# Three edits to an attention and two-MoE kernel: attention ranks, planned cost of the activation sums, address of the stationary operands

## The chip, the cores and the metric

The kernel runs on one core of a Trainium2 chip. The metric is the device time of one execution in microseconds (us). TensorE (PE) does matmuls, and its weight loads (PEld) overlap with them; VectorE is DVE, ScalarE is ACT, GpSimd is POOL, and SyncE (SP) issues all DMAs.

## The reference, cut to what matters

```python
def reference(**kwargs):
    attn_out = _attn_ref(q, k, v)          # 2 x 8 heads, 576 positions, head size 64
    x = attn_out.transpose(0, 2, 1, 3).reshape(1152, 512)
    x = _moe_ref(x, w_gate, w1, w2)         # 8 experts
    return _moe2_ref(x, domain_probs, w1, w2)   # 4 experts

def _attn_ref(q, k, v):
    # softmax attention over positions averaged in fours, repeated four times,
    # plus softmax attention in a window of 7 positions (|i - j| < 4)
    return out_up + out_local

def _moe_ref(x, w_gate, w1, w2):
    P = np.exp(logits - logits.max())       # then 8 rounds of row and column normalisation
    for e in range(8):
        out += P[:, e:e + 1] * (np.maximum(x @ w1[e], 0.0) @ w2[e])   # 512 -> 1024 -> 512
    return out
# _moe2_ref: the same with 4 experts and p = domain_probs / row sum
```

## The kernel before, in words

**Numbers.** Activations and weights are held as a high and a low part in a rounded 32-bit format, and each product is three matmuls (high x high, high x low, low x high).

**Stages.** Attention works on eight pairs of heads and writes `xh` and `xl`, the transposed activations. Twelve experts follow, each in two halves (`grp`). A half has a first product (288 columns of moving activations per matmul, stationary weights `w1s` or `w1s_b`; lines 288, 449, 486) and a second one (512 columns of moving `w2s`, stationary hidden activations `ht`; line 653). The first product uses a recursive scheme with seven products in place of eight, so it needs sums of blocks of activations: one level made by `x_sums` (`sh`, `sl`) and a second by `deep_sums` (`sx` and freed places of the other tiles). A sum is two or more elementwise adds on POOL or DVE (lines 1102, 1108, 1158) and a `keep`: an ACT copy to the high part (line 1172; line 1118 in `x_sums`) and a DVE subtraction for the low part.

**Order.** No queue is written by hand. `Plan.add` records a task with an engine, an estimated cost, what it reads and writes, and a due time: the PE time planned so far, plus `slack`. While an attention pair is recorded, `slack` also takes the next of the 44 values of `plan.ranks` (line 1031). `Plan.run` then simulates the engines with those costs. At each step it takes, per engine, the task that can begin earliest, and among equals the one due first. The order so found is the order in each engine's queue, and on the chip each engine runs its queue strictly in that order. There are two plans: the first (attention, half of expert 0's first half) and the second (the rest), which starts with the engines' simulated times of the first.

**The 44 ranks**, by place: 0 and 1 the two POOL adds that average q and k (lines 872, 874); 2 to 8 the windowed scores; 9 to 21 the averaged scores (19 the POOL multiply of line 923); 22 to 24 the normalisation (24 the POOL multiply of line 857); 25 and 26 the two POOL adds that average v (lines 881, 884); 27 to 33 transposes; 34 to 43 values and the split into `xh` and `xl`. The buffers between 0 and 1, and between 25 and 26, are rings of one.

**Costs of sums.** A POOL add of 288 columns is planned at `pool_cost(288)` = 160 + 2.25 x 288 = 808 ns, a DVE one with both inputs in SBUF at `SHARED` = 870 ns.

**Addresses.** `shifted` (line 252) makes a tile 64 floats longer and starts 36 floats in, that is 144 bytes. `own` holds `ht`, four slots of `w1s` and four of `w2s` one behind the other, all with sizes that are multiples of 256 bytes; `w1s_b` is made by `shifted` too. Unshifted, these tiles begin on a multiple of 256 bytes. So all stationary operands of the experts and the moving `w2s` are at 144 of 256; the moving `xh`, `xl`, `sh`, `sl` and `sx` are at 0 or 128 of 256.

Of the kernel before, what the change touches and what calls it, by code (L numbers as in the profile page):

```python
# [9 lines left out]
F32R = mybir.dt.float32r  # L10
# [189 lines left out]
def tile_attention_moe_moe(  # L200
# [13 lines left out]
    nc = tc.nc  # L214
    NPAIR = qk.shape[0]
    S = qk.shape[2] // 2
    NT, DM = out.shape
    HP = DM // 128
    D = 64
    E1, E2 = w1a.shape[0], w1b.shape[0]  # L220
# [7 lines left out]
    U = S // 2  # L228
# [3 lines left out]
    big = ctx.enter_context(tc.tile_pool(name="big", bufs=1))  # L232
# [18 lines left out]

    def shifted(pool, name, n):

        return pool.tile([128, 64 + n], F32R, name=name)[:, 36:36 + n]

    def w1_slots(t):
        return [x.rearrange("p (a k b) -> p a k b", a=2, k=2) for x in slots(t)]

    def w2_slots(t):
        return [x.rearrange("p (a d) -> p a d", a=2) for x in slots(t)]  # L260

    def slots(t):
        return [t[:, j:j + 1024] for j in range(0, t.shape[1], 1024)]

    own = shifted(big, "own", 8 * NT + 8192)
    ht = own[:, 0:8 * NT].rearrange("p (j a n) -> p j a n", j=4, a=2)
    w1s = w1_slots(own[:, 8 * NT:8 * NT + 4096])
    w2s = w2_slots(own[:, 8 * NT + 4096:])
    acc = [big.tile([128, DM], F32, name=f"acc_{n}") for n in range(3)]
    raw = [big.tile([128, DM], F32, name=f"raw_{j}") for j in range(4)]  # L270

# [6 lines left out]
    plan = Plan()  # L278
# [14 lines left out]
    def copy_cost(n):  # L293
        return 190.0 + 0.85 * n

    def pool_cost(n):
        return 160.0 + 2.25 * n
# [91 lines left out]
    T_OF = {(0, 0): (0, 1, 2), (0, 1): (2, 3, 4), (1, 0): (4, 5, 6), (1, 1): (6, 7, 8)}  # L389
    A_OF = {1: ("x", 1, 0), 2: ("x", 1, 2), 4: ("x", 0, 2), 5: ("s", 0), 6: ("s", 1), 7: ("s", 2), 3: ("s", 3)}  # L390
    DEEP = (3, 7, 5, 4, 6, 2, 1)
    SUMS = (2,2,2,1)
    ON_POOL = (0, 2)

    def ready(g, grp, more=0):
        return sum(SUMS[:max(2 * (g % E1) + grp - (g < E1) + more, 0)])


    def x_tiles(b, u, h=None):
# [26 lines left out]
    def part_of(p, k, u):  # L426

        kind, i, *rest = A_OF[p]
        if kind == "x":
            c = i * S + u * U  # L430
            return [a[:, rest[0] + k, c:c + U] for a in (xh, xl)]
        return [a[:, i, k, u * U:u * U + U] for a in (sh, sl)]

    def part_keys(p, u):
        kind, i, *rest = A_OF[p]
        if kind == "x":
            return x_tiles(i, u, rest[0] // 2)
        return [("s", i, j, hl) for j in (2 * u, 2 * u + 1) for hl in range(2)]
# [585 lines left out]
    def warm(n):  # L1024
# [4 lines left out]


    plan.ranks = (
# [4 lines left out]
    )  # L1036
    for i in range(NPAIR):
        plan.step = 0
# [28 lines left out]
    late = ctx.enter_context(tc.tile_pool(name="late", bufs=1))  # L1067
    late.tile([128, 112], F32, name="gap2")
    w1s += w1_slots(shifted(late, "w1s_b", 1024 * 2))
    raw += [late.tile([128, DM], F32, name=f"raw_{j}") for j in range(4, 6)]  # L1070

# [6 lines left out]
    plan = Plan()  # L1078
# [3 lines left out]


    r_sum = Ring([late.tile([128, U], F32, name=f"sum_{j}") for j in range(3)])
    SHARED = 870.0
    LAG = 18000.0

    def x_sums(j, on_pool=False):

        wd = S // 4  # L1090
        c = wd * j
        part = [[r_tmp.new() for _ in range(2)] for _ in range(2)]

        def v(t):
            return t.slot.rearrange("p (k t) -> p k t", k=2)

        for b in (1, 0):
            o = b * S + c
            tiles = range(o // 128, (o + wd - 1) // 128 + 1)
            for h in range(2):  # L1100
                t = part[b][h]
                plan.add("POOL", pool_cost(2 * wd), lambda t=t, o=o, h=h: nc.gpsimd.tensor_tensor(
                    out=v(t), in0=xh[:, 2 * h:2 * h + 2, o:o + wd].bitcast(F32),
                    in1=xl[:, 2 * h:2 * h + 2, o:o + wd].bitcast(F32), op=ALU.add), [("x", n, h) for n in tiles], (t,))

        def two(dst, x, y, op):
            e = nc.gpsimd if on_pool else nc.vector
            plan.add("POOL" if on_pool else "DVE", pool_cost(2 * wd) if on_pool else SHARED, lambda: e.tensor_tensor(
                out=v(dst), in0=v(x), in1=v(y), op=op), (x, y), (dst,))

        (a21, a22), (a11, a12) = part
        two(a22, a21, a22, ALU.add)
        two(a21, a11, a21, ALU.subtract)
        two(a11, a22, a11, ALU.subtract)
        two(a12, a12, a11, ALU.subtract)
        for i, t in enumerate((a22, a11, a21, a12)):
            hi, lo = sh[:, i, :, c:c + wd], sl[:, i, :, c:c + wd]
            plan.add("ACT", copy_cost(2 * wd), lambda t=t, hi=hi: nc.scalar.activation(
                out=hi, in_=v(t), func=ACTF.Copy), (t,), (("s", i, j, 0),), after=own_keys("s", i))
            plan.add("DVE", SHARED, lambda t=t, hi=hi, lo=lo: nc.vector.tensor_tensor(  # L1120
                out=lo, in0=v(t), in1=hi.bitcast(F32), op=ALU.subtract),
                (t, ("s", i, j, 0)), (("s", i, j, 1),), after=own_keys("s", i))
# [3 lines left out]
    def own_keys(kind, i=None):  # L1126
        return [("l2", p, i_, hl) for (p, i_), (k, j) in homes.items() if k == kind and (i is None or i == j)
                for hl in range(2)]
# [3 lines left out]
    for p in DEEP:  # L1132
        kind, i, *_ = A_OF[p]
        own = (part_of(p, 0, 1), kind, i if kind == "s" else (i, 1, _[0] // 2))
# [7 lines left out]
    def home_keys(p, i):  # L1142

        kind, j = homes[p, i]
        if kind == "s":
            return [("s", j, t, hl) for t in (2, 3) for hl in range(2)]
        if kind == "x":
            return x_tiles(*j)
        return []

    def deep_sums(p, on_pool):

        pool = (nc.gpsimd, "POOL", pool_cost(U))
        t = [r_sum.new() for _ in range(3)]

        def sub(eng, dst, x, y, reads, writes, op=ALU.subtract, slack=LAG, after=()):
            e, name, cost = eng
            plan.add(name, cost, lambda: e.tensor_tensor(  # L1158
                out=dst(), in0=x(), in1=y(), op=op), reads, writes, slack=slack, after=after)

        def whole_part(d, u, k):
            hi, lo = part_of(p, k, u)
            sub(pool, lambda: d.slot, lambda: hi.bitcast(F32), lambda: lo.bitcast(F32), part_keys(p, u), (d,), ALU.add)

        def two(dst, x, y, op):
            sub(pool if on_pool else dve, lambda: dst.slot, lambda: x.slot, lambda: y.slot, (x, y), (dst,), op)

        dve = (nc.vector, "DVE", SHARED)

        def keep(i, d):  # L1170
            hi, lo = sums[p][i]
            plan.add("ACT", copy_cost(U), lambda: nc.scalar.activation(
                out=hi, in_=d.slot, func=ACTF.Copy), (d,), (("l2", p, i, 0),), after=home_keys(p, i), slack=LAG)
            sub(dve, lambda: lo, lambda: d.slot, lambda: hi.bitcast(F32), (d, ("l2", p, i, 0)), (("l2", p, i, 1),),
                after=home_keys(p, i))

        whole_part(t[0], 1, 0)
        whole_part(t[1], 1, 1)
        whole_part(t[2], 0, 0)
        two(t[1], t[0], t[1], ALU.add)  # L1180
        two(t[0], t[2], t[0], ALU.subtract)
        two(t[2], t[1], t[2], ALU.subtract)
        keep(0, t[1])
        keep(2, t[0])
        keep(1, t[2])
        whole_part(t[1], 0, 1)
        two(t[1], t[1], t[2], ALU.subtract)
        keep(3, t[1])
# [171 lines left out]
    for q in range(2):  # L1360
        for h in range(2):
            for u in range(2):
                plain_unit(first_w1[2 * h:2 * h + 2], q, 2 * q + h, 1, u)
        for j in range(2):
            x_sums(2 * q + j, 2 * q + j in X_POOL0)
# [9 lines left out]
    def tiles(g, grp, w):  # L1375
# [54 lines left out]
        for i, n in enumerate(ORDER):  # L1430
            if i in SUM_AT and ready(g, grp) + SUM_AT.index(i) < ready(g, grp, 1):
                work.append(lambda k=ready(g, grp) + SUM_AT.index(i): deep_sums(DEEP[k], k in ON_POOL))
            if special and i:
                work.append(lambda i=i: whole_tile(i))
            elif i < (4 if 1 in DEEP[:ready(g, grp, 1)] else 5):
                work += steps(i)
            else:
                rest += steps(i)
# [115 lines left out]
```

## Time and profile before

| | us |
|---|---|
| median of 3 runs | 1172.27 (1172.06 to 1172.35) |
| the profiled execution | 1173.12 |
| its span, first to last instruction | 1171.3 |
| PE busy in the span | 1157.0 |
| POOL busy | 950.7 |
| DVE busy | 838.9 |
| ACT busy | 656.1 |

The profiled execution took 1.8 us outside its span, and was 0.85 us longer than the median of the runs. Matmuls are pipelined and their recorded ends are modelled, so a PE that is 99% busy may still wait: what one matmul costs is read from the chain of waits, where a piece with its count runs from the first start to the next piece. The mean TensorE clock granted was 0.999 of 2.4 GHz.

### The profile page before, as it was taken

The page shows a single profiled execution, that of the slowest core. Times are in us where ns is not written, and L with a number is a line of the kernel's source. Part 1 is how long each engine was busy: PE and PEld are TensorE (multiplying, and loading weights), DVE is VectorE, ACT ScalarE, POOL GpSimd, SP SyncE. Part 2 cuts the span into 40 slices and gives each one's busy share as a digit, 9 for nine tenths or more (in the row PEclk, how much of TensorE's full clock was granted, in tenths as well). Part 3 has the DMA queues.
Part 4 walks back from the last instruction along what each step waited for, and adds up shares of the span by engine and source line. Part 5 has one row for each costly group of instructions (what it writes and reads, how often), then busy time and mean ns, then how long its engine had stood idle before and what let it go on. Part 6 is the DMA issues. An engine that isn't in the chain of part 4 may idle for free.

```text
span 1171.3 us, 21868 instructions
## 1 busy us (share of the span) xinstructions
PE 1157.0 (99%) x7419; PEld 1030.2 (88%) x7419; DVE 838.9 (72%) x1777; ACT 656.1 (56%) x1614; POOL 950.7 (81%) x1045
## 2 busy tenths in 40 slices
PE   8999999999999999999999999999999999999998
PEld 6788998988988988988988988989888888898897
DVE  6867878888767667667667568566787887776764
ACT  4754435745655655655655656545454565575561
POOL 7978768898898798898898898749888889879870
PEclk9999999999999999999999999999999999999999
DMA  7613335444555545544544554641235445555544
GB/s 214 187 63 109 117 127 169 146 157 149 189 160 170 176 153 169 173 156 164 183 155 159 184 162 153 189 144 37 90 108 174 133 162 171 163 171 171 157 159 144
DMA packets 97632, 179.20 MB, mean 153 GB/s; under 512 B 12336, under 2 KB 13104, under 8 KB 97520
## 3 DMA queue, kind: packets, MB, share of 16 engines
q1 hardware_dynamic: 97520, 177.81, 47.6%
q8 instruction: 58, 0.95, 0.3%
q14 instruction: 54, 0.44, 0.1%
HBM read 123.50 MB, written 54.26 MB: 152 GB/s over the span
## 4 chain that ended last, share of the span: by engine, by line
PE 91%; POOL 4%; DVE 2%; DMA 1%; issue 1%; ACT 0%; SPq 0%; POOLq 0%; ACTq 0%; DVEq 0%
PE bank L653 48%; PE bank L486 30%; PE bank L449 6%; PE bank L288 4%; POOL raw L337 2%; POOL own L310 1%; DMA v<-in_v_dram 1%; POOL sum L1158 1%; PE bank L731 1%; PE bank L829 0%; DMA raw<-in_w1b_dram 0%; DVE sum L1158 0%; PE bank L1225 0%; PE bank L1197 0%; POOL w1s_b L310 0%
## 5 line engine op out<-in xcount | busy, mean ns | idle before, releaser
L653 PE MATMUL bank<-own 128*128 128x512 f32 (+1 forms) x2604 | 664.0, 391 | 0.0
L653 PEld LDWEIGHTS bank<-own 128*128 128x128 f32 x2604 | 464.6, 188 | 75.5
L310 POOL TENSOR_TENSOR own<-raw,own 128x512 fp32r<-128x512 f32 (+1 forms) x291 | 357.1, 1242 | 78.1 <-ACT own L308 70.3
L464 DVE TENSOR_TENSOR bank<-bank,tmp 128x288 f32<-128x288 f32 x502 | 207.7, 458 | 145.2 <-ACT bank L506 80.7
L337 POOL TENSOR_TENSOR raw<-raw,raw 128x128 f32<-128x128 f32 (+1 forms) x346 | 242.4, 702 | 20.1 <-DMA raw<-in_w1a_dram 2.7
L506 ACT ACTIVATE bank<-bank 128x288 f32<-128x288 f32 x387 | 153.1, 396 | 126.1 <-PE bank L486 122.1
L308 ACT ACTIVATE own<-raw 128x512 fp32r<-128x512 f32 (+1 forms) x291 | 168.6, 595 | 68.3 <-POOL raw L337 50.6
L698 DVE SCALAR_TENSOR_TENSOR acc<-bank,prob,acc 128x512 f32<-128x512 f32 (+1 forms) x190 | 138.9, 741 | 90.5 <-DMA acc<-out_dram 57.4
L302 ACT ACTIVATE tmp<-bank 128x288 f32<-128x288 f32 x217 | 86.9, 411 | 115.6 <-PE bank L486 96.3
L464 DVE TENSOR_TENSOR tmp<-bank,tmp 128x288 f32<-128x288 f32 x340 | 137.3, 449 | 5.6 <-PE bank L486 3.6
L310 POOL TENSOR_TENSOR w1s_b<-raw,w1s_b 128x384 fp32r<-128x384 f32 (+1 forms) x96 | 114.1, 1196 | 27.3 <-ACT w1s_b L308 27.2
L406 ACT ACTIVATE own<-bank 128x288 fp32r<-128x288 f32 x296 | 111.7, 410 | 42.4 <-DVE bank L464 27.9
L408 DVE SCALAR_TENSOR_TENSOR own<-bank,own 128x288 fp32r<-128x288 f32 x296 | 117.1, 446 | 13.2 <-ACT own L406 12.9
L337 POOL TENSOR_TENSOR raw<-raw 128x256 f32<-128x256 f32 x129 | 100.4, 778 | 31.7 <-PE bank L653 11.1
L486 PE MATMUL bank<-sh,own 128*128 128x288 f32 x408 | 109.0, 295 | 0.0
L486 PE MATMUL bank<-sx,own 128*128 128x288 f32 x603 | 107.8, 297 | 0.0
L486 PE MATMUL bank<-xh,own 128*128 128x288 f32 x374 | 100.9, 295 | 0.0
L486 PEld LDWEIGHTS bank<-sx,own 128*128 128x128 f32 x603 | 92.8, 189 | 5.9 <-ACT bank L506 0.8
L486 PEld LDWEIGHTS bank<-sh,own 128*128 128x128 f32 x408 | 74.9, 188 | 4.4
L486 PEld LDWEIGHTS bank<-xh,own 128*128 128x128 f32 x374 | 69.0, 188 | 3.8
L308 ACT ACTIVATE w1s_b<-raw 128x384 fp32r<-128x384 f32 (+1 forms) x96 | 53.9, 576 | 28.7 <-POOL raw L337 26.0
L408 DVE SCALAR_TENSOR_TENSOR own<-tmp,own 128x288 fp32r<-128x288 f32 x88 | 66.7, 814 | 0.3 <-ACT own L406 0.3
(150 smaller groups left out, 1635.3 us busy)
## 6 DMA issues: line engine op xcount, KB each, us to landing
out_dram<-acc SPq DMA_DIRECT2D x206, 256.0 KB, 2.0
acc<-out_dram SPq DMA_DIRECT2D x198, 256.0 KB, 2.8
raw<-in_w1a_dram SPq DMA_DIRECT2D x94, 256.0 KB, 2.9
raw<-in_w2a_dram SPq DMA_DIRECT2D x64, 256.0 KB, 2.7
raw<-in_w1b_dram SPq DMA_DIRECT2D x46, 256.0 KB, 2.8
raw<-in_w2b_dram SPq DMA_DIRECT2D x32, 256.0 KB, 3.1
qk<-in_qk_dram SPq DMA_DIRECT2D x7, 576.0 KB, 7.3
vw<-in_vw_dram SPq DMA_DIRECT2D x8, 320.0 KB, 6.9
```

The costliest lines, as they stand in the source:

```text
L302: nc.scalar.activation(out=dst(), in_=src(), func=ACTF.Copy, **kw)
L308: plan.add("ACT", copy_cost(n), lambda: nc.scalar.activation(out=hi(), in_=src(), func=ACTF.Copy), keys, ((b, 0, 0),))
L310: plan.add("POOL", pool_cost(n), lambda: nc.gpsimd.tensor_tensor(out=lo(), in0=src(), in1=hi().bitcast(F32), op=ALU.subtract), (*keys, (b, ...
L337: plan.add("POOL", pool_cost(n), lambda: nc.gpsimd.tensor_tensor(out=out(), in0=x(), in1=y(), op=op), keys, (key,))
L406: plan.add("ACT", c0[0], lambda: nc.scalar.activation(out=ht[:, s, 0, c:c + U], in_=src(), func=ACTF.Relu), (key,), ((*k, 0),), slack=slack)
L408: plan.add("DVE", c0[1], lambda: nc.vector.scalar_tensor_tensor(out=ht[:, s, 1, c:c + U], in0=src(), scalar=0.0, in1=ht[:, s, 0, c:c + U]. ...
L449: nc.tensor.matmul(out=ps.slot[:, 0:U], lhsT=w.slot[:, j, k, 128 * (1 - q):128 * (1 - q) + 128], rhs=a[hl], start=(first and k == 0 and n ...
L464: plan.add("DVE", cost, lambda: nc.vector.tensor_tensor(out=get(dst), in0=get(ps), in1=get(b), op=ALU.add), tuple({ps, b} - {dst}), (dst,) ...
L486: nc.tensor.matmul(out=view(ps), lhsT=b.slot[:, j].rearrange("p k b -> p (k b)")[:, c:c + 128], rhs=a[hl], start=(first and n == 0), stop= ...
L506: nc.scalar.activation(out=view(dst), in_=view(src), func=ACTF.Copy)
L653: nc.tensor.matmul(out=ps.slot[:, 0:nd], lhsT=ht[:, j, a, 128 * n:128 * n + 128], rhs=w[j].slot[:, b, c0:c0 + nd], start=(j == 0 and p == ...
L698: plan.add("DVE", 130 + 1.2 * nd, lambda: nc.vector.scalar_tensor_tensor(out=a(), in0=ps.slot[:, 0:nd], scalar=prob[:, n, e:e + 1], in1=a( ...
```

## The change

New values for the 44 ranks; POOL's adds for the activation sums are planned at 860 ns (`PARTS`) and DVE's at 910 ns (`SHARED`); `shifted` starts 60 floats (240 bytes) in, and `w2s` becomes a tile of its own, unshifted, placed ahead of `own`, so it lies at 0 of 256. `SUMS` becomes two tuples with the old values each, which selects the same numbers.

```diff
     def shifted(pool, name, n):
-        return pool.tile([128, 64 + n], F32R, name=name)[:, 36:36 + n]
+        return pool.tile([128, 64 + n], F32R, name=name)[:, 60:60 + n]
...
-    own = shifted(big, "own", 8 * NT + 8192)
+    w2s = w2_slots(big.tile([128, 4096], F32R, name="w2s"))
+    own = shifted(big, "own", 8 * NT + 4096)
     ht = own[:, 0:8 * NT].rearrange("p (j a n) -> p j a n", j=4, a=2)
-    w1s = w1_slots(own[:, 8 * NT:8 * NT + 4096])
-    w2s = w2_slots(own[:, 8 * NT + 4096:])
+    w1s = w1_slots(own[:, 8 * NT:])
...
-    SUMS = (2,2,2,1)
+    SUMS = (2, 2, 2, 1), (2, 2, 2, 1)
...
-        return sum(SUMS[:max(2 * (g % E1) + grp - (g < E1) + more, 0)])
+        return sum(SUMS[g >= E1][:max(2 * (g % E1) + grp - (g < E1) + more, 0)])
...
     plan.ranks = (
-        -1500, 500, 4400, 3700, 4900, 9800, -1000, -9500, 200, -1800, 800, 3500,
-        4200, -1000, -2000, 2600, 3200, -17900, -16300, 3600, -12500, -27100, 3800, 3500,
-        -12900, 3500, -3200, 2200, 1400, 10500, -17800, -5800, 2300, -35600, -30400, -1600,
-        -2200, -20500, -17700, -17500, -39100, 5500, -15400, -10200,
+        -5600, 23700, -8900, 7700, 1000, 18700, 2200, -40900, 10700, -35200, 800, 3500, 0, -2000, -4500, 300,
+        5200, -25700, -29300, -5600, -6900, -32600, 8800, 7600, -8900, -17500, 13000, -13300, -4600, 11200, -13000, -10700,
+        8400, -31200, -46600, -17700, -500, -30000, -14100, -24000, -42100, 4100, -35900, 3800,
     )
...
-    SHARED = 870.0
+    SHARED, PARTS = 910.0, 860.0
...
-                plan.add("POOL", pool_cost(2 * wd), lambda t=t, o=o, h=h: nc.gpsimd.tensor_tensor(
+                plan.add("POOL", PARTS, lambda t=t, o=o, h=h: nc.gpsimd.tensor_tensor(
...
-            plan.add("POOL" if on_pool else "DVE", pool_cost(2 * wd) if on_pool else SHARED, lambda: e.tensor_tensor(
+            plan.add("POOL" if on_pool else "DVE", PARTS if on_pool else SHARED, lambda: e.tensor_tensor(
...
-        pool = (nc.gpsimd, "POOL", pool_cost(U))
+        pool = (nc.gpsimd, "POOL", PARTS)
```

## Rows read from the trace of the kernel before

**Rows 1.** The page, part 1: busy time, share and instructions of each engine

```profile
PE 1157.0 (99%) x7419; PEld 1030.2 (88%) x7419; DVE 838.9 (72%) x1777; ACT 656.1 (56%) x1614; POOL 950.7 (81%) x1045
```

**Rows 2.** Windows: length, busy PE, PEld, DVE, ACT, POOL, clock, DMA share, GB/s

```profile
20.00:48.00 28.00, 27.10 (x539) 21.23 (x533) 24.27 (x61) 21.29 (x64) 27.02 (x30) 1.00 0.64 182
48.00:82.00 34.00, 32.65 (x363) 28.26 (x362) 22.68 (x54) 20.89 (x56) 26.80 (x30) 1.00 0.23 79
...
140.00:778.00 638.00, 637.83 (x3655) 570.25 (x3654) 456.44 (x984) 374.71 (x919) 530.79 (x587) 1.00 0.51 164
838.00:845.00 7.00, 4.17 (x22) 3.94 (x21) 4.17 (x6) 4.63 (x13) 6.74 (x8) 0.76 0.28 105
```

**Rows 3.** The same windows' PE and PEld for lines 288, 449, 486, 653, in turn

```profile
0.00:1172.00 1172.00, 54.24 (x384) 51.30 (x384) 1.00 0.48 153
...
0.00:1172.00 1172.00, 83.58 (x600) 81.95 (x600) 1.00 0.48 153
...
0.00:1172.00 1172.00, 425.00 (x2709) 402.27 (x2709) 1.00 0.48 153
...
0.00:1172.00 1172.00, 664.02 (x2604) 464.59 (x2604) 1.00 0.48 153
```

**Rows 4.** Chain of waits in pieces: start us, length us, what, count of instructions

```profile
81.84 4.34 PE bank L1225 x24
...
201.25 9.52 PE bank L449 x72
...
214.35 1.61 PE bank L486 x12
...
235.13 11.73 PE bank L653 x51
...
800.84 20.55 PE bank L288 x156
...
841.19 11.07 PE bank L449 x72
```

**Rows 5.** Weight loads by line and shape: busy us, mean ns, idle before

```profile
L653 PEld LDWEIGHTS bank<-own 128*128 128x128 f32 x2604 | 464.6, 188 | 75.5
...
L1329 PEld LDWEIGHTS bank<-prob,ones 128*128 128x128 f32 x16 | 2.7, 188 | 0.3
```

**Rows 6.** Windows 20:48 and 48:82, the warm-up matmuls of line 731 alone

```profile
20.00:48.00 28.00, 4.14 (x48) 3.07 (x48) 1.00 0.64 182
48.00:82.00 34.00, 0.99 (x14) 0.82 (x14) 1.00 0.23 79
```

**Rows 7.** Timeline of POOL at the end of attention: start, length, what, idle before

```profile
51.64 0.67 POOL L874 TENSOR_TENSOR qkd<-t 128x288 f32<-128x288 f32 x1
...
54.71 5.01 POOL L310 TENSOR_TENSOR own<-raw,own 128x512 fp32r<-128x512 f32 x4
...
72.42 6.68 POOL L1102 TENSOR_TENSOR tmp<-xh,xl 128x288 f32<-128x288 f32 x8 [6.77 <-ACT xh L1015]
```

**Rows 8.** Timeline of PE: the wait at 52 us and the gate's matmuls

```profile
52.36 0.71 PE L897 MATMUL bank<-qkd 64*72 64x144 f32 x8 [0.67 <-POOL qkd L874]
...
81.84 0.35 PE L1225 MATMUL bank<-xh,wg_a 128*16 128x384 f32 x1 [0.69 <-ACT acc L692]
```

**Rows 9.** Timeline of ACT around 838 us

```profile
837.98 0.44 ACT L1172 ACTIVATE sh<-sum 128x288 fp32r<-128x288 f32 x1 [4.78 <-POOL sum L1158]
...
840.17 0.67 ACT L688 ACTIVATE acc<-bank,prob 128x512 f32<-128x512 f32 x1
840.74 0.70 ACT L302 ACTIVATE tmp<-bank 128x288 f32<-128x288 f32 x2
```

**Rows 10.** Waits of PE from 100 to 970 us: total us, times, longest

```profile
PE bank L449 <- ACT tmp L302: 2.8, 1, 2.8
PE bank L486 <- ACT bank L506: 2.1, 4, 1.0
```

**Rows 11.** Line 1158, the deep sums: ns min/median/max, first and last start

```profile
L1158 DVE TENSOR_TENSOR sum<-sum,sum x40: 442/746/1546, 154.3 to 975.3; 128x288 f32<-128x288 f32 x40
...
L1158 POOL TENSOR_TENSOR sum<-sh,sl x32: 796/820/1039, 110.8 to 900.2; 128x288 f32<-128x288 f32 x32
```

## The prediction, made before the changed kernel was run

> **What bounds the kernel now.** I read the busy times first, then the windows, then the chain of waits. PE is recorded as busy for 1157.0 of 1171.3 us [rows 1], and in the steady stretch from 140 to 778 us for 637.83 of 638.00 [rows 2]: there, nothing but PE's own pace counts, and POOL, at 530.79, has room. Since the ends of matmuls are modelled, the pace itself has to be taken from the chain, where length over count is the distance from one matmul to the next. A 512-column one takes 11.73 / 51 = 230.0 ns. A 288-column one takes 20.55 / 156 = 131.7, 9.52 / 72 = 132.2 or 1.61 / 12 = 134 ns, say 132.4 [rows 4]. There are 384 + 600 + 2709 = 3693 of 288 columns and 2604 of line 653 [rows 3]. So the experts cost about 3693 x 0.1324 + 2604 x 0.2300 = 489 + 599 = 1088 us of PE, and 83 us of the span are something else: the attention before the experts, some transposes, and a few stalls. A change can only act on (a) the pace per matmul, (b) the first 82 us, (c) the stalls.
>
> **Part 1, the address of the stationary operands** acts on (a). Nothing is added or removed; 3693 + 2604 = 6297 matmuls and as many weight loads get other addresses. At 2.4 GHz, one column a cycle, 512 columns are 213.3 ns and 288 are 120.0, so the excess is 16.7 ns for 512 and 11.7 to 14 for 288 [rows 4]; all excess together is about 2604 x 16.7 + 3693 x 12.4 = 89 us. What of it hangs on addresses the trace of before cannot show directly, for every stationary operand is at 144 of 256. Two readings bound it.
> First, the 512-column matmuls are those whose moving operand, `w2s`, shares the residue 144 with the stationary one, and they have the larger excess; after the change no moving operand shares it. If the whole difference to 12.0 ns came from that, the gain is 4.7 x 2604 = 12.2 us. Against this: the gate's matmuls of 384 columns, whose moving `xh` is at 0, take 4.34 / 24 = 180.8 ns, an excess of 20.8 over 160.0 [rows 4], so a larger excess with more columns does not need a shared residue. That end is far off.
> Second, an isolated load takes 188 ns from `own` at 144 and 188 ns from `ones`, which lies at 0 of 256 [rows 5]: the load itself does not care. That speaks for nothing at all.
> On the loss side, the runs of 288 columns that have no wait spread over 131.7 to 134 ns; if all 6297 moved by half of that spread, 1 ns, it would be 6.3 us in either direction. I take a sixth of the larger gain, -2 us, as the nearer row (the 384 columns) says most of the excess is length; the ends are -12 and +6.
> The Trainium skill ("TensorE: Matmul & The Clock Gate", "Step-by-step: what each phase is for") says that PE reads moving and stationary operands through two independent SBUF ports, so that loading the next weights steals nothing from the running matmul. By that rule this part is worth 0 instead of -2, which is the first rival below. The equal 188 ns agree with it; the uneven excess neither shows nor excludes it.
>
> **Part 2, longer planned costs of the sums** acts on (c). On the chip nothing gets longer: the planner only believes that a POOL sum takes 860 instead of 808 ns and a DVE one 910 instead of 870, so everything that reads a sum gets a later place in its engine's queue. The measured sums are 796/820/1039 ns on POOL and 442/746/1546 on DVE (min/median/max) [rows 11]; the new figures lie above both medians and below the slow ones, so they are more cautious, not more exact. Where it matters is a queue that stands behind a sum. Around 838 us ACT stood 4.78 us before a `keep` (line 1172), for which POOL's sum was late; queued behind it were a tile's scaling (line 688) and the eviction of line 302 [rows 9]. PE waited 2.8 us for that eviction [rows 10], and after it the clock had fallen: 0.76 on the mean of 838 to 845 us [rows 2], so the next 72 matmuls took 11.07 instead of 9.52 us [rows 4], 1.55 more. Four more waits, 2.1 us in all, are for line 506, another ACT copy [rows 10]. The sum of what a better order could give back is 2.8 + 1.55 + 2.1 = 6.4 us.
> How much of it? Ahead of that `keep` lie 24 POOL adds of `x_sums` (16 of line 1102 and 8 of line 1108) and some seven of `deep_sums`; 31 x 52 ns = 1.6 us by which the planner now sees it later, a third of the 4.78 us by which it was early. So I take a third of 6.4, -2 us. The ends: -6.4, and, as the same shift can put some other copy in front of an eviction elsewhere, one more event like that at 838 us, +4.4. Behind a `keep` that waits are always ACT's evictions, and PE waits for those as soon as the banks or scratch tiles run out.
>
> **Part 3, the ranks** act on (b). They add and remove no instruction, they only break ties between tasks that can begin at once, in the first plan alone. SP's queue keeps its order there; what can move are the times at which its loads find a free buffer. From 20 to 48 us POOL is busy 27.02 of 28.00 us and PE 27.10 [rows 2], with 4.14 us of that (48 matmuls) warm-up [rows 6]; from 48 to 82 us warm-up is 0.99 us. PE's real work is thus nearly solid from 20 us on, and no order can bring back more than the warm-up: -4.14 - 0.99 = -5 us. Many of those warm-ups are written into the kernel and stay, so I take -1. POOL's places move most: rank 0 falls by 4100 and rank 25 by 21000 (the first adds on q, k and v earlier, which frees v's buffers for the next load earlier), ranks 1 and 26 rise by 23200 and 16200 (the second adds later). Loss: second rival, +8.
>
> **The sum.** Span 1171.3 + 1.8 outside = 1173.1 for the profiled execution; -2 - 2 - 1 = -5 gives 1168.1. The profiled execution lies 0.85 above the median of the runs, so the median to expect is 1172.3 - 5.0 = 1167.3 us.
>
> **The rivals.**
> (1) No effect: loads run beside the moving operand whatever their address, the `keep` at 838 us stays ahead of the eviction (1.6 us of shift against 4.78), and PE's solid stretch from 20 us stays as it is, so only the order in attention changes, by less than 1 us. For it: the equal 188 ns [rows 5]. Against it: two of the three parts would have to miss. Time: 1171.5, between 1170 and 1174.
> (2) Slower, through POOL's queue in attention. With rank 1 at +23700, the second add of q and k (line 874) of the last pairs is due behind the eight splits of weights (line 310, no rank), which take 5.01 / 4 = 1.25 us each. Before, the add at 51.64 us went ahead of six of them, the first four at 54.71 [rows 7], and even so PE waited 0.67 us for it at 52.36 [rows 8]. Behind six, it is 7.5 us later, and so are the last pair's averaged scores, its values and the end of attention. The gate's matmuls begin at 81.84 us, while POOL's first activation sum, which needs the last `xh`, began at 72.42 [rows 7, 8]: some 9 us cover for the gate, none for the sums, on which POOL is then behind. It decides if more than about 2 of the 7.5 us reach the sums; I price it at 7.5 less 2.5 of cover from units of line 288: +5, with the other two parts at half, 1172.3 + 5 - 2 = 1175.
> (3) Slower, through the pace: 240 is the worse residue by 1 ns a matmul, +6.3, with -3 from the rest: 1175.6. Nothing in the rows favours a sign for 288 columns.
> (4) Much faster: the shared residue of `w2s` and `ht` was the cause of the larger excess: -12.2, with -1 from the rest, 1159.
>
> **How the numbers follow.** The forecast, with its own range of 1163 to 1170, has 0.45; (1) 0.20; (2) 0.12; (3) 0.10; (4) 0.13. About 0.2% is what a measurement of this kernel can tell from no change, 2.3 us: faster means under 1169.9, slower over 1174.6. The forecast and (4) are faster, 0.58; (1) is the same, 0.20; (2) and (3) are slower, 0.22. The range has to reach (4) and the centre of (2) and (3) with some of what lies above: 1158 to 1177.
>
> **What the profile of the changed kernel would show.** Part 1: in the chain, a run of line 653 at or under 229 ns a matmul where it was 230.0, and runs of lines 288 and 449 under 131.5. If these are the same to 0.2 ns, part 1 gave nothing and the Trainium skill's rule stands. Part 2: no ACT `keep` with a wait over 4 us near 838 us, no clock under 1.00 between 838 and 845 us, and a shorter list of PE's waits for lines 302 and 506. Part 3: the gate's matmuls before 81 us; by rival (2) after 83, with the second adds on POOL behind the splits. The prediction is wrong if the stretch from 140 to 778 us becomes longer, or if a new wait of more than 3 us shows on PE after 100 us.

## The result, and the profile after

The changed kernel takes 1159.16 us (1158.80 to 1160.73) against 1172.31 us for the kernel before beside it: a ratio of 0.9886, interval 0.9868 to 0.9904, or 13.1 us less. The forecast was 1167.3, so the direction was right and the gain is 2.6 times what was forecast. The profiled execution of after took 1158.8 us with a span of 1157.0, so 14.3 us have gone from the span of 1171.3.

The page of after, part 1, answers to [rows 1]. POOL, DVE and ACT do the same work in the same time; only the span is shorter.

```profile
PE 1147.8 (99%) x7399; PEld 1026.3 (89%) x7399; DVE 832.6 (72%) x1777; ACT 656.8 (57%) x1614; POOL 948.7 (82%) x1045
```

**Attention** ends earlier. The first of the gate's matmuls (line 1224 of after, 1225 of before) began at 81.84 us [rows 8] and now does at 76.70, which is 5.1 us. Timeline of PE, after (start, length, what, and in brackets the idle time before and its releaser, where there is any):

```profile
76.70 0.34 PE L1224 MATMUL bank<-xh,wg_a 128*16 128x384 f32 x1
```

**The pace** is better. Pieces of the chain of waits of after (start, length, what, count), beside [rows 4]:

```profile
197.50 9.56 PE bank L449 x72
...
793.42 20.73 PE bank L288 x156
...
1087.07 8.85 PE bank L653 x39
```

and the same unbroken run of line 653 in the kernel before:

```profile
1100.86 8.97 PE bank L653 x39
```

It fell from 230.0 to 226.9 ns a matmul, while lines 288 and 449 even rose, from 131.7 to 132.9 and from 132.2 to 132.8. I therefore took, from both traces, the distance from each matmul's start to the next (leaving out those with a wait), and grouped it:

| mean distance, ns | before | after | count |
|---|---|---|---|
| 512 columns, in unbroken runs over 24 | 230.1 | 227.3 | about 1110 |
| 512 columns, between groups of line 486 | 230.6 | 230.7 | about 1455 |
| 288 columns, line 486 | 132.9 | 131.8 | 2709 |
| 288 columns, line 449 | 132.2 | 132.4 | 600 |
| 288 columns, line 288 | 131.9 | 132.3 | 384 |

That is 1110 x 2.8 + 2709 x 1.1 = 6.1 us less in two of five groups and some 0.4 us more in the others, 5.7 us in all.

**The stalls** behind the gate fell by 3.5 us, from 15.7 to 12.2, when all distances between matmuls over the usual ones are added up. PE's waits from the gate to 1000 us in after (us, times, longest), beside [rows 10]:

```profile
PE bank L449 <- ACT tmp L302: 3.0, 2, 1.6
```

The four waits for line 506 (2.1 us) are gone, and the one of 2.8 us for line 302 has become two shorter ones, of which one is new. The rest shows on ACT. Timeline of ACT in after around the place of [rows 9]:

```profile
830.67 0.44 ACT L1171 ACTIVATE sh<-sum 128x288 fp32r<-128x288 f32 x1 [4.76 <-POOL sum L1157]
831.02 0.67 ACT L688 ACTIVATE acc<-bank,prob 128x512 f32<-128x512 f32 x1
831.59 0.43 ACT L1171 ACTIVATE xh<-sum 128x288 fp32r<-128x288 f32 x1
831.92 0.40 ACT L302 ACTIVATE tmp<-bank 128x288 f32<-128x288 f32 x1
832.50 0.45 ACT L1171 ACTIVATE xh<-sum 128x288 fp32r<-128x288 f32 x1 [0.18 <-POOL sum L1157]
```

The first copy of a sum still stands 4.76 us, as before (4.78). In the kernel before, two more copies stood between it and the tile's scaling:

```profile
838.86 0.44 ACT L1172 ACTIVATE xh<-sum 128x288 fp32r<-128x288 f32 x1 [0.43 <-POOL sum L1158]
839.82 0.44 ACT L1172 ACTIVATE xh<-sum 128x288 fp32r<-128x288 f32 x1 [0.52 <-POOL sum L1158]
```

Now the scaling has passed both, and the first eviction of line 302 has passed one of them, so PE gets its scratch tile earlier. After this shorter wait the clock stayed up. Windows of after (columns as in [rows 2]), with 1.00 where [rows 2] had 0.76:

```profile
140.00:778.00 638.00, 637.95 (x3676) 572.16 (x3675) 457.14 (x982) 375.09 (x918) 527.14 (x586) 1.00 0.52 165
...
830.00:838.00 8.00, 6.52 (x46) 5.95 (x46) 4.54 (x7) 4.93 (x14) 7.69 (x9) 1.00 0.25 93
```

So 5.1 + 5.7 + 3.5 = 14.3 us, all that has gone from the span: each of the three parts gave more than it was given in the sum.

### The profile page after: what moved, and what is told of

Its sections match the earlier page's. It is cut to its first block, busy times and chain, and to the rows that moved or that the text cites. A ratio compares the mean times of both kernels' runs of the same rounds, so it can differ in the third digit from the quotient of the medians.

```text
span 1157.0 us, 21831 instructions
## 1 busy us (share of the span) xinstructions
PE 1147.8 (99%) x7399; PEld 1026.3 (89%) x7399; DVE 832.6 (72%) x1777; ACT 656.8 (57%) x1614; POOL 948.7 (82%) x1045
## 4 chain that ended last, share of the span: by engine, by line
PE 92%; POOL 4%; DMA 2%; DVE 1%; ACT 0%; issue 0%; SPq 0%; ACTq 0%; POOLq 0%; DVEq 0%
PE bank L653 48%; PE bank L486 31%; PE bank L449 6%; PE bank L288 3%; POOL tmp L1101 1%; POOL sum L1157 1%; DMA qk<-in_qk_dram 1%; DMA v<-in_v_dram 1%; DVE sl L1119 1%; POOL tmp L1107 0%; POOL own L310 0%; PE bank L989 0%; POOL raw L337 0%; PE bank L829 0%; PE bank L979 0%
## 5 line engine op out<-in xcount | busy, mean ns | idle before, releaser
L653 PE MATMUL bank<-w2s,own 128*128 128x512 f32 (+1 forms) x2604 | 661.4, 391 | 0.0
L653 PEld LDWEIGHTS bank<-w2s,own 128*128 128x128 f32 x2604 | 464.3, 188 | 71.9
L464 DVE TENSOR_TENSOR bank<-bank,tmp 128x288 f32<-128x288 f32 x502 | 208.0, 457 | 132.2 <-ACT bank L506 70.5
L310 POOL TENSOR_TENSOR own<-raw,own 128x384 fp32r<-128x384 f32 (+1 forms) x195 | 232.8, 1205 | 36.1 <-ACT own L308 34.6
L310 POOL TENSOR_TENSOR w2s<-raw,w2s 128x512 fp32r<-128x512 f32 x96 | 124.4, 1318 | 31.3 <-ACT w2s L308 26.9
L308 ACT ACTIVATE own<-raw 128x384 fp32r<-128x384 f32 (+1 forms) x195 | 108.9, 580 | 66.6 <-POOL raw L337 56.1
L337 POOL TENSOR_TENSOR raw<-raw 128x256 f32<-128x256 f32 x129 | 100.4, 778 | 38.1 <-PE bank L653 13.7
```

What stands on the lines that cost most here:

```text
L308: plan.add("ACT", copy_cost(n), lambda: nc.scalar.activation(out=hi(), in_=src(), func=ACTF.Copy), keys, ((b, 0, 0),))
L310: plan.add("POOL", pool_cost(n), lambda: nc.gpsimd.tensor_tensor(out=lo(), in0=src(), in1=hi().bitcast(F32), op=ALU.subtract), (*keys, (b, ...
L337: plan.add("POOL", pool_cost(n), lambda: nc.gpsimd.tensor_tensor(out=out(), in0=x(), in1=y(), op=op), keys, (key,))
L464: plan.add("DVE", cost, lambda: nc.vector.tensor_tensor(out=get(dst), in0=get(ps), in1=get(b), op=ALU.add), tuple({ps, b} - {dst}), (dst,) ...
L653: nc.tensor.matmul(out=ps.slot[:, 0:nd], lhsT=ht[:, j, a, 128 * n:128 * n + 128], rhs=w[j].slot[:, b, c0:c0 + nd], start=(j == 0 and p == ...
```

## The experiments

All ratios are to the kernel before, run beside the experiment on the same chip, with 95% intervals. Of two profiled executions, of `e8_parts` and `e13_no_ranks`, the first 82 us ran partly at the lower clock; what is read from them lies behind that stretch.

**One part at a time.** The new ranks on the kernel before:

```diff
     plan.ranks = (
-        -1500, 500, 4400, ...
+        -5600, 23700, -8900, ...
```

> The kernel before with the new ranks alone. Theory (the three parts add up, each at what the traces of before and after show): the gate's first matmul, at 81.84 us before and 76.70 after, comes at 76.7, the pace stays at 230.4 and 132.7 ns a matmul, the wait near 838 us stays within 1 us of before; time 1172.3 - 5.1 = 1167.2, between 1166 and 1169. Rival (the earlier start is given back later, since the second plan starts from other engine times): the gate at 76.7 too, but new waits after 82 us eat over 3 us; 1170 to 1173.

Measured: 0.9964 (0.9947 to 0.9981), 4.2 us less. The gate's first matmul came at 78.5 us, the pace was 230.4 and 132.7. Some of the gain is indeed given back: a wait called "near 110 us" here (on PE it lies between 115 and 118 us), of which the weight load shows 1.0 us and the matmul behind it 0.8, is in no kernel with the old ranks. The profiled execution, 1171.77 us, is the slowest of the ten of this kernel.

The planned costs alone:

```diff
-    SHARED = 870.0
+    SHARED = 910.0
...
-                plan.add("POOL", pool_cost(2 * wd), ...
+                plan.add("POOL", 860.0, ...
```

> The kernel before with only the planned costs of the sums raised (860 and 910 ns). Theory: attention and pace as before (gate at 81.8 us, 230.4 and 132.7 ns), the wait of ACT at the copy of a sum near 838 us shrinks under 2 us and the clock stays up; PE's stalls after 82 us fall by some 3 us; 1169.3, between 1167 and 1171. Rival (the cost alone moves the copies by 1.6 us of 4.8 and changes nothing; the stalls changed because attention ends elsewhere): 1171.5 to 1173.

Measured: 0.9946 (0.9924 to 0.9968), 6.3 us less, more than either expected. The first copy near 836 us still waits, and yet the evictions come through as in after. Timeline of ACT, costs alone:

```profile
835.80 0.44 ACT L1172 ACTIVATE sh<-sum 128x288 fp32r<-128x288 f32 x1 [4.83 <-POOL sum L1158]
836.15 0.67 ACT L688 ACTIVATE acc<-bank,prob 128x512 f32<-128x512 f32 x1
836.72 0.43 ACT L1172 ACTIVATE xh<-sum 128x288 fp32r<-128x288 f32 x1
837.05 0.40 ACT L302 ACTIVATE tmp<-bank 128x288 f32<-128x288 f32 x1
```

PE's waits with costs alone, from 100 to 970 us, 1.9 us where [rows 10] had 4.9:

```profile
PE bank L449 <- ACT tmp L302: 1.4, 1, 1.4
PE bank L486 <- ACT bank L506: 0.5, 1, 0.5
```

Counting all distances between matmuls over the usual ones behind the gate, stalls fell from 15.7 to 11.1 us (transposes of some 3 to 4 us are in both). The wait for line 302 gives 1.4 us of it, the waits for line 506 give 1.6, and the clock, which stayed at 1.00 behind them, gives the 1.55 of [rows 4]. The 4.6 us are thus accounted for; what is left to 6.3 us lies within the interval.

The costs of POOL's sums alone, and of DVE's alone, are the two halves of that edit:

> The kernel before with only POOL's sums planned longer (860 ns), DVE's left at 870. Theory: the wait near 838 us is for POOL's sums, so this carries most of the gain of both costs (0.54%): stalls after the gate fall from 15.7 to about 12 us, time 0.3 to 0.55% less. Rival (the copies behind DVE's sums, near 255, 897 and 941 us, carry it): under 0.15% less, stalls 14.5 to 16.

> The kernel before with only DVE's sums planned longer (910 ns), POOL's left at 808. Theory (with POOL's costs alone 0.31%, with both 0.54%): this alone gives the rest, 0.1 to 0.3%, and the wait near 838 us stays, since it is for POOL's sums. Rival (the planner's order is a matter of luck, any change of a cost gives another one): outside 0 to 0.4%, or the wait near 838 us changes by over 1 us.

Measured: 0.9969 (0.9950 to 0.9988) for POOL's, with stalls of 11.6 us, and 0.9979 (0.9968 to 0.9989) for DVE's, with stalls of 13.7 us. They add up to the whole (0.31 + 0.21 against 0.54%). With DVE's alone PE still waits 2.3 us for line 302, with POOL's 1.4, so the shorter wait near 838 us is mostly POOL's matter, as expected. Not expected is that the clock stays at 1.00 from 838 to 845 us with DVE's costs alone too, so the place is not POOL's alone.

The addresses alone:

```diff
-        return pool.tile([128, 64 + n], F32R, name=name)[:, 36:36 + n]
+        return pool.tile([128, 64 + n], F32R, name=name)[:, 60:60 + n]
...
+    w2s = w2_slots(big.tile([128, 4096], F32R, name="w2s"))
+    own = shifted(big, "own", 8 * NT + 4096)
```

> The kernel before with only the addresses changed: stationary operands at 240 of 256, the second product's weights in a tile of their own at 0. Theory (the pace hangs on addresses): 229.2 ns for 512 columns and 132.0 for 288, as in the kernel after, so 2604 x 1.2 + 3693 x 0.7 = 5.7 us less; 1166.6, between 1165 and 1168. Rival (the pace in the kernel after is a matter of which engines run beside PE, not of addresses): the pace stays at 230.4 and 132.7, 1172 within 1.

Measured: 0.9955 (0.9935 to 0.9975), 5.3 us less, with 229.2 and 132.0 ns as in after. Everything else was as before, and the stalls were 16.8 us: the pace hangs on addresses. The kernel after with the old addresses was not run, so what they are worth beside the other two parts is known from the paces alone.

**Which address.** Seven kernels place the stationary operands and the second product's weights (`w2s`, moving) differently. Two are the kernel before with one edit: `w2s` taken out to 0 with 36 floats kept, and 36 replaced by 60 with `w2s` left in `own`. Five are the kernel after with another number of floats in `shifted`, as in

```diff
-        return pool.tile([128, 64 + n], F32R, name=name)[:, 60:60 + n]
+        return pool.tile([128, 64 + n], F32R, name=name)[:, 12:12 + n]
```

> The kernel before with the second product's weights in a tile of their own at 0 of 256, and the stationary operands left at 144. Theory (the moving operand's address counts: it no longer shares the stationary one's residue): 512 columns at 229.2 ns, 288 columns unchanged at 132.7, so 3.1 us less, 1169.2. Rival (the stationary operand's address counts): 512 columns at 230.4 or slower, 1172 or more.

> The kernel before with 60 in place of 36 floats in the shifted tiles: stationary operands and the second product's moving weights all at 240 of 256. Theory D (what counts is the distance of the stationary address from the moving one, modulo something): line 653 has distance 0 as before and stays at 230.4 ns, the 288-column matmuls have the distances of the kernel after and take 132.0; 1172.3 - 2.6 = 1169.7 against a before of 1172.3. Rival S (the stationary address alone counts): 229.2 and 132.0 as in the kernel after, 1166.6. Rival M (the moving address at 0 is needed for the gain): 230.4 and 132.7 or worse.

> The kernel after with 12 in place of 60 floats: stationary operands at 48 of 256, which has the same place in a line of 64 bytes as 240. Theory D64 (only the place within 64 bytes counts): 229.2 and 132.0 ns as in the kernel after, its time within 0.2%. Rival D256 (the whole residue counts): one of the two paces moves by more than 0.4 ns, 2 us or more.

> The kernel after with no shift: stationary operands and second-product weights at 0 of 256. Theory D: distance 0 for line 653, so 230.4 ns as before, 3.1 us more than the kernel after; the 288-column matmuls get distances 0 and 128 in place of 240 and 112, unknown, 132 to 134. Time 0.2 to 0.8% above the kernel after. Rival S: both paces change together by more than 1 ns.

> The kernel after with 32 in place of 60 floats: stationary operands at 128 of 256, the second product's weights at 0. So far, with those weights at 0: stationary at 0 gave 229.2 and 132.2 ns, 240 gave 229.2 and 132.0, 48 gave 233.1 and 132.9, 144 gave 232.7 and 132.8. Theory P128 (the pattern repeats every 128 bytes, so 128 is like 0): 229.2 and 132.2, ratio to before 0.988 to 0.990. Rival P256 (the whole residue counts): 512 columns at 231 or more, ratio 0.992 or more.

> The kernel after with 4 in place of 60 floats: stationary operands at 16 of 256, the second product's weights at 0. Theory N (addresses near the moving one's residue are good): 229.2 to 229.6 ns for 512 columns and 132.0 to 132.3 for 288, ratio 0.988 to 0.990. Rival (good is only what begins at or just ahead of a multiple of 256): 231 or more, like 48.

> The kernel after with 56 in place of 60 floats: stationary operands at 224 of 256, the second product's weights at 0. Theory N: 229.2 to 229.6 and 132.0 to 132.3 ns, ratio 0.988 to 0.990. Rival (240 is a place of its own): 231 ns or more for 512 columns, ratio 0.992 or more.

| stationary, `w2s` at (of 256) | 512 columns, all, ns | in long runs | 288 columns, all | ratio to before |
|---|---|---|---|---|
| 144, 144 (before) | 230.4 | 230.1 | 132.7 | 1 |
| 144, 0 (`e5_w2s0`) | 232.7 | 233.1 | 132.8 | 1.0029 (1.0012 to 1.0045) |
| 240, 240 (`e4_all240`) | 232.2 | 232.6 | 132.0 | 1.0006 (0.9987 to 1.0024) |
| 240, 0 (after) | 229.2 | 227.3 | 132.0 | 0.9886 (0.9868 to 0.9904) |
| 0, 0 (`e7_st0`) | 229.3 | 227.4 | 132.2 | 0.9895 (0.9878 to 0.9912) |
| 16, 0 (`e15_st16`) | 232.8 | 232.5 | 132.7 | 0.9982 (0.9964 to 1.0000) |
| 48, 0 (`e6_st48`) | 233.1 | 233.2 | 132.9 | 0.9998 (0.9988 to 1.0007) |
| 128, 0 (`e12_st128`) | 232.0 | 232.3 | 132.6 | 0.9964 (0.9949 to 0.9978) |
| 224, 0 (`e16_st224`) | 232.6 | 233.2 | 133.0 | 0.9978 (0.9968 to 0.9988) |

The last five have the new ranks and costs as well, so their ratios stand against after, the paces against all. The run of 39 matmuls of line 653 shows it in one line of the chain each; `e4_all240`:

```profile
1100.03 9.09 PE bank L653 x39
```

`e7_st0`:

```profile
1090.60 8.86 PE bank L653 x39
```

Every simple rule that was put up has fallen. It is not the distance of the two addresses (`e4_all240` keeps before's distance of 0 for line 653 and is 1.8 ns slower), not the stationary address alone (the same kernel keeps after's 240), not the place in 64 bytes (48 is not like 240) and not in 128 (128 is not like 0). With `w2s` at 0, only 0 and 240 of the seven places tried are good, and their neighbours 16 and 224 are as bad as the rest: 2.8 to 3.9 ns more than 240 for a matmul of 512 columns. By the ratios the kernels after with 16, 48, 128 or 224 lose 9 to 13 us of the 13.1. No shift at all does what 240 does, within 0.1%.

For 288 columns two kernels with 144 agree (132.7 and 132.8) and so do two with 240 (132.0), wherever `w2s` lies. That the place of the stationary operands sets the pace is shown, since the five kernels after with another shift differ from after in nothing else. For `w2s` it is less clean: taken out of `own` it comes to lie ahead of `ht` and `w1s`, so its place in the memory changes together with its residue, and the two were not tried apart. Why the paces differ is open.

**What the ranks do.** Only POOL's six places changed:

```diff
-        -1500, 500, 4400, 3700, ...
+        -5600, 23700, 4400, 3700, ...   (places 0, 1, 19, 24, 25, 26 new)
```

> The kernel before with the new ranks at POOL's six places alone (0, 1, 19, 24, 25, 26), the other 38 as before. Theory (the order on POOL is the gain: v's first add earlier, so v's buffers and the loads behind them come earlier): the gate's first matmul at 77 to 79 us, time 0.25 to 0.45% less, as with all ranks (0.36%). Rival (PE, DVE and ACT must follow the new order too): less than half of it, under 0.15%, or slower.

Measured: 0.9982 (0.9971 to 0.9992), half the gain of all ranks, with the gate at 78.6 us, as early as with all of them. Neither expectation holds whole: POOL's order counts. Whether the other 38 places add to it is not shown, since the interval overlaps that of all ranks. The wait near 110 us is absent.

**Leaving one part out.** The kernel after with the old ranks, and with the old planned costs:

> The kernel after with the old ranks: costs and addresses alone. Theory (the new ranks end attention earlier but bring a wait of 1.5 to 2.4 us near 110 us, seen in every kernel with all new ranks and in none with the old ones): that wait is under 0.6 us here, the gate's first matmul at 79.5 to 82 us; ratio to before 0.990 to 0.992, so the ranks are worth 0.1 to 0.3% beside the others and not 0.36%. Rival (the parts simply add up, and the difference is noise): 0.990 or less with the wait near 110 us as in the kernel after.

> The kernel after with the old planned costs of the sums, 808 and 870 ns: ranks and addresses alone. Theory: the wait for the eviction near 832 us is back at 3 us or more, with a clock under 1.00 there, and so are the waits near 251 and 941 us; ratio to before 0.991 to 0.994. Rival (with the new ranks the second plan starts from other times, and the costs do not matter): 0.989 or less.

Measured: 0.9914 (0.9887 to 0.9942) without the ranks, 0.9930 (0.9911 to 0.9950) without the costs, against 0.9886. Beside the others the ranks are worth about 0.28% and the costs 0.44%, each a little less than alone, though the intervals overlap. For the ranks even that may be too much: of the four executions without them, two had a granted clock under 1.000 (0.993 and 0.996), and the two at 1.000 took 1160.4 and 1161.1 us, some 1.6 us more than after. Without the ranks the wait near 110 us is not there. It is of the known kind; timeline of ACT in after:

```profile
113.58 0.44 ACT L1171 ACTIVATE xh<-sum 128x288 fp32r<-128x288 f32 x1 [6.75 <-POOL sum L1157]
```

Without the costs, the old state of 838 us is back, now near 834 us: PE waits 2.7 us for the eviction (3 or more were expected) and 2.1 us in four waits for line 506, and the clock falls. Timeline of ACT and, in the second fence, a window of `e14_no_costs`:

```profile
831.50 0.45 ACT L1171 ACTIVATE sh<-sum 128x288 fp32r<-128x288 f32 x1 [4.65 <-POOL sum L1157]
```

```profile
834.00:841.00 7.00, 6.28 (x36) 6.28 (x37) 5.03 (x9) 5.40 (x15) 5.16 (x7) 0.76 0.24 71
```

**One step further.** Since POOL's weight work is planned too short as well, its cost was raised too, in the kernel after:

```diff
+    slow = [160.0, 2.25]
...
-        return 160.0 + 2.25 * n
+        return slow[0] + slow[1] * n
...
+    slow[:] = 200.0, 2.3
```

> The kernel after with all of POOL's other work in the second plan planned longer as well, 200 + 2.3 n ns for 160 + 2.25 n (1378 for 1312 at 512 columns, where the trace of before has 1326 to 1332, 494 for 448 at 128, where it has 487). Theory (what remains of the wait near 832 us is POOL's weight work, which the planner takes to be shorter than it is, ahead of the sums): ACT's first copy of a sum there waits under 3 us in place of 4.76 and PE's waits there are under 1 us; 1 to 3 us less than the kernel after, ratio to before 0.985 to 0.9885. Rival (luck of the order): slower than the kernel after, ratio over 0.990.

Measured: 0.9964 (0.9944 to 0.9984), 9 us slower than after. The theory is right on the spot and wrong for the whole, where the rival, luck of the order, came in. Timeline of ACT, and PE's longest wait (lines are two further down here):

```profile
834.32 0.45 ACT L1174 ACTIVATE sh<-sum 128x288 fp32r<-128x288 f32 x1 [1.54 <-POOL sum L1160]
```

```profile
PE bank L488 <- ACT sx L1174: 3.5, 1, 3.5
```

The copy near 834 us waits 1.54 us in place of 4.76, and stalls of 0.5 us are left there where after has 2.2. But between 920 and 940 us another copy of a sum was late, with 6.8 us of stalls, and more near 110 and 250 to 300 us: 23.0 us behind the gate against 12.2.

## Why the prediction was right and wrong, step by step

**What bounds the kernel** was right: the steady stretch moved by the pace and nothing else, and POOL's, DVE's and ACT's work is what it was. One slip changes nothing: 24 of the 2604 matmuls of line 653 have 256 columns.

**Part 1, the address**, was taken at -2 us and is worth -5.3 alone (6 by the paces). The step that failed is the choice of a sixth of the gain. It rested on the 384-column matmuls, read as proof that the excess is length. Their 180.8 ns were misread: the 4.34 us hold the whole last matmul, and from the first start to the last it is 4.00 us for 23 distances, 174 ns, an excess of 14.0 and not 20.8. And their stationary operand has 16 columns and lies elsewhere, so they were no control for either reading. The equal 188 ns of two isolated loads [rows 5] misled too: after also has 188 ns, and runs faster. The thought that `w2s` and `ht` share a residue was also wrong as a cause: taking `w2s` away from it alone (`e5_w2s0`) made line 653 slower by 2.3 ns, and in after only the long runs got faster. What stands in its place: with everything else equal, the address of the stationary operands alone moves the long runs from 227.3 to 233.2 ns (240 against 48, 0 for `w2s`). The Trainium skill ("TensorE: Matmul & The Clock Gate", "Step-by-step: what each phase is for") says that PE reads the two operands through independent ports, so that loading the next weights takes no read bandwidth from the running matmul. By that rule, as the prediction used it, this part would be 0. The runs differ from that, and the measurement decides; whether it is the load that holds up the matmul, no run here shows.

**Part 2, the costs**, was taken at -2 us, with -6.4 as the far end, and is worth 4.6 us of stalls and -6.3 by the times. Place and mechanism were right: the copy near 838 us, the eviction behind it, the lost clock and the four waits for line 506. The term was a third of 6.4, because 1.6 us of shift is a third of the 4.78 us of wait. That proportion is the mis-sized step: an order is not shifted in proportion. The first copy did not move (4.76 us still, where the prediction had named a wait under 4 us as its sign), but it was enough that the scaling passed two copies and the eviction one: the wait for it fell to 1.4 us with the costs alone, and the clock stayed at 1.00, which saved another 1.55.

**Part 3, the ranks**, was taken at -1 us with -5 as the end; the runs give -4.2 alone and about 0.28% beside the others, and the two profiles 5.1. The step that failed is the bound: it let an order bring back nothing but warm-up matmuls behind 20 us. That its -5 was near the 5.1 is luck. Those warm-ups only fell from 5.13 to 4.15 us; what fell more is PE's idle time before the gate, from 6.2 to 2.8 us, most of it in the first 20 us, which the bound had left out. Windows of before and after (columns as in [rows 2]):

```profile
0.00:20.00 20.00, 16.09 (x280) 13.72 (x283) 11.83 (x41) 6.51 (x16) 12.52 (x24) 1.00 0.83 238
...
0.00:20.00 20.00, 18.45 (x328) 15.68 (x331) 13.26 (x45) 8.86 (x23) 14.21 (x26) 1.00 0.87 250
```

Part of the 5.1 is no merit of the order, since the end of attention differs between executions: in six kernels with the old ranks the gate began between 79.7 and 81.9 us, 80.6 in the mean, in nine with the new ones between 76.1 and 79.1, 77.3 in the mean. The first 20 us differ between executions as well, so which wait the ranks shorten in all of them stays open; what all nine have in common is 126 warm-up matmuls before the gate where all kernels with the old ranks have 146.

**The rivals.** (1), no effect, is out on all three parts. (2), the second add of q and k behind the splits of weights, did not come: the splits ran behind it. (3) is out for 240, but its price was of the right size: with `w2s` at 0, the wrong residues are 1.6 to 2.7 ns per 512 columns slower than before, 4 to 8 us by the paces, and in the kernels after they took 9 to 13 us, most or all of the gain. (4) gave a time close to the measured one, 1159, by luck: its reason, the shared residue, is refuted by `e5_w2s0`, and the time came from all three parts.

**The sum.** Alone the parts give 4.2 + 6.3 + 5.3 = 15.8 us, together 13.1. The difference of 2.7 us lies within the intervals; the wait near 110 us that the new ranks bring, 2 us in after, would account for most of it. Against the terms -2, -2 and -1 of the sum stand 5.3, 6.3 and 4.2: all three were mis-sized, the second with the right mechanism, the first without a cause that holds and the third under a bound that does not. The own range of the forecast, 1163 to 1170, was too narrow because all three terms were taken at the low end at once, each with the argument that its bound is far off.

## What to carry to other kernels

Here the stall behind a strictly ordered queue was a matter of order, not of amount: look at which instruction stands ahead of the one that PE waits for, and ask whether the change lets that one pass, not by how much it shifts. And in `e11_poolcost` planned costs nearer to the measured ones made the kernel 9 us slower, so such a correction is to be measured, not trusted.

Take the pace per matmul from the starts, apart for runs and mixed stretches, before calling PE-bound time fixed: two addresses were worth half a per cent here, and a place 16 bytes further, 16 for 0 or 224 for 240, cost 0.9%.

## What the runs showed of the hardware that was not expected

The distance between matmuls depends on where the stationary operand lies within 256 bytes: with `w2s` at 0, from 227.3 to 233.2 ns for 512 columns in long runs, and 132.0 to 133.0 for 288. The recorded weight load is 188 ns in before and after alike, so it does not show the difference. The placing of the moving `w2s` counts too: from 230.1 to 233.1 ns when it alone was taken out of `own`.

In two of eight profiled executions with the old ranks the clock went to the lower level within attention, and in a third (`e3_addr`) for a short time (0.91 as the mean of 20 to 40 us); in none of nine with the new ones it did. Windows of `e13_no_ranks`, the kernel after with the old ranks:

```profile
20.00:25.00 5.00, 3.16 (x71) 2.46 (x67) 2.81 (x8) 3.40 (x13) 4.91 (x5) 0.99 0.85 192
25.00:40.00 15.00, 14.96 (x171) 11.39 (x173) 7.99 (x20) 6.47 (x19) 10.21 (x11) 0.50 0.70 195
```

and of after:

```profile
20.00:25.00 5.00, 4.73 (x95) 3.64 (x95) 4.61 (x12) 3.99 (x11) 4.48 (x6) 1.00 0.90 241
25.00:40.00 15.00, 14.37 (x302) 11.48 (x302) 13.63 (x36) 11.74 (x34) 14.64 (x16) 1.00 0.83 222
```

After a stretch with PE busy for 3.16 of 5 us, the clock granted was 0.50 (1.2 GHz) for 15 us, in which PE got through 171 matmuls where after did 302, and the gate began at 87.3 us, some 7 us late. The new order was busy for 4.73 of the same 5 us and kept 2.4 GHz. Whether the order is the reason, these profiles cannot settle. The times of all executions point that way: 10 of 149 with the old ranks had a mean clock of 0.994 or less (`e8_parts` and `e13_no_ranks` have 0.992 and 0.993 in their profiles), and none of 62 with the new ones. Where in the kernel the unprofiled ones lost it is not recorded.
